# Decode attention and token mixer on one core: the order of the V loads that stay, and three resident V chunks ahead of K

## The chip, the cores and the metric

The kernel runs on one core of a Trainium2 chip, in one launch. The metric is the device time of that launch in microseconds (us), less is better; the time of a kernel is the median of its runs. The core's engines are called PE (matrix products), DVE (vector), ACT (scalar functions), POOL and SP; here SP only issues the loads, one after the other, each when its target cell is free.

## The reference

```python
def _A_ref(x, k_cache, v_cache, wq, wo):      # Hq = 32, Hkv = 8, Sk = 32768, Dh = 128, D = 512, B = 2
    q = (x @ wq).reshape(B, 1, 32, 128).transpose(0, 2, 1, 3)
    k, v = jnp.repeat(k_cache, 4, axis=1), jnp.repeat(v_cache, 4, axis=1)
    p = softmax(einsum("bhqd,bhkd->bhqk", q, k) * 128 ** -0.5)
    o = einsum("bhqk,bhkd->bhqd", p, v)
    return o.transpose(0, 2, 1, 3).reshape(B, 1, 4096) @ wo
def _B_ref(x, w1, b1, w2, b2):                 # S = 1 token, F = 1792
    u = gelu(einsum("bsd,sf->bdf", layernorm(x), w1) + b1)
    return (einsum("bdf,fs->bds", u, w2) + b2).transpose(0, 2, 1)

x = x + _A_ref(layernorm(x), k_cache, v_cache, wq, wo)
x = x + _B_ref(layernorm(x), w1, b1, w2, b2)
x = x + _A_ref(layernorm(x), k_cache, v_cache, wq, wo)   # the same caches and weights again
x = x + _B_ref(layernorm(x), w1, b1, w2, b2)
```

All in float32. The caches are 2 x 8 heads of 32768 x 128 for K and for V, and both layers read all of them.

## The kernel before

**Units and chunks.** A unit is one layer, one batch and one KV head: 32 of them, numbered 0 to 31 in the order of the list `units`. Each has 8 chunks of K and 8 of V; a chunk is 4096 keys, 128 partitions x 4096 floats, 2.097 MB. Head 7 is the keeper: parts of its K and V stay on the chip from layer 0 to layer 1. Unit 13 (N1) is layer 0, batch 0, head 7; unit 14 is layer 0, batch 1, head 5; unit 15 is layer 1, batch 0, head 7; unit 16 (N2) is layer 0, batch 1, head 7; unit 17 is layer 1, batch 0, head 5; unit 18 (N3) is layer 1, batch 1, head 7; unit 19 is layer 1, batch 1, head 5. At units 13 and 16 a batch's layer 0 ends (a "change"): the output goes through the mixer, and the query of a unit two later comes from it.

**The stream.** A list `stream` holds all loads with a key, and its sorted order is the order of everything: SP issues loads in it and PE takes the chunks in it, so K of one unit and V of the unit before are interleaved. A position is the number of chunks taken so far. `parts` (L857 on) says which chunks a load takes together; `FOLLOWS` (L34) gives V of units 15 and 18 their keys relative to K of the next unit. "K14 2" is chunk 2 of K of unit 14 below, "V1-3" chunks 1 to 3 of V.

**What stays.** `KEPT` gives, for each chunk of the keeper's V, how many of its 8 parts stay and the cell: chunks 1 to 3 in cells 8 to 10, chunks 5 to 7 in cells 3 to 5, and of chunk 4 five eighths in cell 13. The other three eighths of chunk 4 are loaded into a half cell; two of them are copied by DVE into two banks of PSUM (`kept`, L537) and in layer 1 copied back (L526), the third is loaded again. In layer 1, chunks 1 to 3 and 5 to 7 need no load ("resident").

**The cells.** Between units 12 and 19 the loads share the cells 0 to 10, each one chunk, with the weights in 9 to 12. For every load the planner (`spread`, `half`, `fit`, `room`) takes the cells with the largest lead (how many chunks are loaded between the position that frees them and this load, at most 4, and that no later booked use cuts off), and among equals those free first. After the V of units 13 and 16, with chunks 1 to 3 and 5 to 7 in their cells, the next K (L866, one chunk at a time from chunk 2) goes through four half cells, 6.0, 6.5, 7.0 and 7.5 (the number is cell and half), in turn. A half is free when PE has multiplied what was in it, and, where DVE copies from it, when that is done as well.

**The end of a unit.** With the last V chunk taken, DVE adds the blocks (L546, L548), PE turns them (L618), the output product follows (L245). At a change the rows are then copied (L632), go to PE (L664) and through a normalisation, and `hidden_sum` runs 14 tiles through ACT (L803) and DVE (L818, L820), one tile at a time; `mix_3` (L828) takes the sum to PE at the position after K chunk 6. PE works in program order, so these stand between K chunks.

**Scores.** K gives scores in PSUM, two halves of 4 chunks each. After the last K chunk: the maximum (L440, L446, L448, L450, L454, L456), a transposition of each half into `S` (L460), exponentials on ACT (L465), four for each half; V chunks 0 to 3 use the first half, 4 to 7 the second. The query of a unit is made by products (L339), a copy (L361) and a turn (L365) some positions ahead of its K; for unit 19 the copy goes to the memory of `S[0]`, so it stands ahead of the transposition of unit 18's first half, which the program puts 3 positions ahead of K19 at the earliest. `load_weights` (L118) brings two heads' weights in one load; for unit 20 it goes to cells 9 and 10, 7 positions ahead of K20.

Of the kernel before, what the change touches and what calls it, by code (L numbers as in the profile page):

```python
# [30 lines left out]
KEPT_Q = 4  # L31
RESIDENT = (5, 7)
TWO_HEADS = ((0, 1), (2, 3), (4, 6), RESIDENT)
FOLLOWS = {2: (2.2, -0.9, -0.8, -0.7, 3.5, -0.6, -0.5, -0.4), 5: (3.05, 1.1, 1.2, 1.3, 5.1, 3.1, 3.2, 3.3)}  # L34
PIECES = (32, 16, 8, 4, 4)
THIN = 16
QT = 4
# [7 lines left out]
def gqa_mixer_kernel(ctx: ExitStack, tc: tile.TileContext, x, kt, v, wqo, cols, out):  # L45
# [811 lines left out]
    def parts(n, with_v):  # L857

        m = n + with_v
        if m < N1 or n > N3 and m > N3 + 1:  # L860

            loads = ((0, 4), (4, 2), (6, 2)) if m == NU else ((0, 2), (2, 2), (4, 2), (6, 2)) if m == N3 + 2 else GROUPS
            return [(c, k, NCH) for c, k in loads]
        if not with_v:
            loads = ((0, 3), (3, 1), (4, 2), (6, 2)) if n in (N1, N2) else ((0, 2), (2, 2), (4, 2), (6, 2))
            if n in (N1 + 1, N2 + 1):  # L866
                loads = ((0, 2), *((c, 1) for c in range(2, NCH)))
            if n in (N1 + 2, N3):
                loads = [(c, 1) for c in range(NCH)]
        elif n in (N1, N2):  # L870
            loads = ((0, 1), (5, 3), (1, 3), (4, 1))
        elif n in (N1 + 1, N2 + 1):
            loads = [(c, 1) for c in range(NCH)]
        elif n < N1:
            loads = ((0, 2), (2, 2), (4, 2), (6, 2))
        else:
            loads = [(c, 1) for c in range(NCH)]
        return [(c, k, RING) for c, k in loads]

    stream = []  # L880
    for n in range(NU):
        stream += [(n * NCH + c + m - 1, 0, n, c, m, limit) for c, m, limit in parts(n, 0)]
        for i, (c, m, limit) in enumerate(parts(n, 1)):
            if n in (N1, N2):
                key = (n + 1) * NCH + 1 + (i + 1) / (2 * NCH)
            elif n in (N1 + 1, N2 + 1):
                key = (n + 1) * NCH - 0.5 + max(c / (2 * NCH) - 0.5, c - 2 + m)
            elif n - N1 in FOLLOWS:
                key = (n + 1) * NCH + FOLLOWS[n - N1][c]
            else:  # L890
                key = (n + 1) * NCH + c + m - 1 + (LAG if N1 - 1 <= n <= N3 else 0)
            stream.append((key, 1, n, c, m, limit))
# [215 lines left out]
```

## Time and profile before

| | us |
|---|---|
| median of 3 runs | 2496.51 |
| lowest and highest of them | 2495.5, 2499.65 |
| the profiled execution | 2498.0 |
| its span in the trace | 2496.2 |
| PE busy / DVE busy / ACT busy | 1374.8 / 240.2 / 187.4 |

The profile lists busy time by engine; groups of instructions by line; the chain of work that ended last, followed backwards from the last instruction; DMA queues; and, by windows, for each stretch the busy time of PE, PE's weight loads, DVE, ACT and POOL with the number of instructions, then PE's granted clock (1.00 is full speed), the mean busy share of the 16 DMA engines (short windows can show more than 1, since a packet counts where it ends) and GB/s. A row of the timeline is: start, duration, engine, line, operation, target and source, count, and in brackets the idle time before and what ended it. A row of the waits is: who waited for whom, total us, times, longest. A timeline row with a count merges several instructions; its duration is then the stretch from the first to the end of the last.

### The profile page before, as it was taken

The page shows a single profiled execution, that of the slowest core. Times are in us where ns is not written, and L with a number is a line of the kernel's source. Part 1 is how long each engine was busy: PE and PEld are TensorE (multiplying, and loading weights), DVE is VectorE, ACT ScalarE, POOL GpSimd, SP SyncE. Part 2 cuts the span into 40 slices and gives each one's busy share as a digit, 9 for nine tenths or more (in the row PEclk, how much of TensorE's full clock was granted, in tenths as well). Part 3 has the DMA queues.
Part 4 walks back from the last instruction along what each step waited for, and adds up shares of the span by engine and source line. Part 5 has one row for each costly group of instructions (what it writes and reads, how often), then busy time and mean ns, then how long its engine had stood idle before and what let it go on. Part 6 is the DMA issues. An engine that isn't in the chain of part 4 may idle for free.

```text
span 2496.2 us, 20457 instructions
## 1 busy us (share of the span) xinstructions
PE 1374.8 (55%) x9270; PEld 373.0 (15%) x9270; DVE 240.2 (10%) x632; ACT 187.4 (8%) x554; POOL 4.9 (0%) x17
## 2 busy tenths in 40 slices
PE   4545445645445544657677666465455464456546
PEld 1111111111111111111121111111111111111112
DVE  1000000000000000003113100000000000010002
ACT  0000000000000000002012000000000000011002
POOL 0000000000000000000000000000000000000000
PEclk8777767876777777778887887777778677777778
DMA  9999999999999999999999999999999999999996
GB/s 420 435 435 427 436 429 436 431 434 431 435 434 431 433 427 431 430 429 388 432 430 401 427 426 430 439 433 431 430 437 430 431 433 433 434 429 433 427 434 279
DMA packets 30336, 1063.04 MB, mean 426 GB/s; under 512 B 3621, under 2 KB 3625, under 8 KB 4522
## 3 DMA queue, kind: packets, MB, share of 16 engines
q1 hardware_dynamic: 29960, 1061.70, 99.0%
q8 instruction: 73, 1.20, 0.2%
q14 instruction: 13, 0.11, 0.0%
q10 hardware_dynamic: 290, 0.04, 0.0%
HBM read 1061.72 MB, written 0.00 MB: 425 GB/s over the span
## 4 chain that ended last, share of the span: by engine, by line
DMA 74%; PE 24%; another core or an unknown queue 0%; issue 0%; DVE 0%; ACT 0%; SPq 0%
DMA mem<-in_v_dram 63%; PE acc L578 19%; DMA mem<-in_kt_dram 12%; PE scores L425 3%; PE small L454 0%; PE small L609 0%; PE rows L245 0%; PE bcast L339 0%; PE small L448 0%; PE kept L760 0%; PE bcast L664 0%; PE bcast L640 0%; DVE S L548 0%; ACT S L465 0%
## 5 line engine op out<-in xcount | busy, mean ns | idle before, releaser
L425 PE MATMUL scores<-mem,small_sb 128*32 128x512 f32 x4096 | 634.8, 739 | 610.0 <-DMA mem<-in_kt_dram 609.9
L578 PE MATMUL acc<-mem,S 128*16 128x512 f32 x4088 | 601.4, 728 | 459.8 <-DMA mem<-in_v_dram 453.4
L425 PEld LDWEIGHTS scores<-mem,small_sb 128*32 128x32 f32 x4096 | 151.4, 129 | 999.2 <-issue 910.3
L465 ACT ACTIVATE S<-S,small_sb 128x128 f32<-128x128 f32 x240 | 123.3, 517 | 2105.5 <-DVE small_sb L456 1630.7
L578 PEld LDWEIGHTS acc<-mem,S 128*16 128x16 f32 x4088 | 133.1, 110 | 819.9 <-issue 694.1
L440 DVE TENSOR_REDUCE small_sb<-scores 128x1 f32<-128x512 f32 x64 | 44.2, 691 | 813.6 <-PE scores L425 813.6
L460 DVE STREAM_TRANSPOSE S<-scores 128x512 f32<-128x512 f32 x64 | 45.4, 710 | 114.6 <-PE acc L578 114.6
L339 PE MATMUL kept<-mem,small_sb 128*2 128x512 f32 x104 | 51.2, 618 | 1.7 <-DVE small_sb L273 1.7
L245 PE MATMUL rows<-mem,small_sb 128*1 128x512 f32 (+1 forms) x276 | 49.0, 605 | 2.6 <-ACT mem L803 2.4
L465 ACT ACTIVATION_READ_ACCUMULATOR S<-S,small_sb 128x1 f32 x240 | 44.8, 187 | 0.0
L611 DVE RECIPROCAL small_sb<-small 128x4 f32<-128x4 f32 x32 | 5.9, 184 | 322.9 <-PE small L609 322.9
L450 DVE TENSOR_REDUCE small_sb<-small 1x4 f32<-1x128 f32 x32 | 8.9, 279 | 277.7 <-PE small L448 277.7
L620 DVE TENSOR_TENSOR small_sb<-small,small_sb 128x4 f32<-128x4 f32 x31 | 5.1, 164 | 295.6 <-PE small L618 295.6
L548 DVE SCALAR_TENSOR_TENSOR S<-acc,small_sb,S 128x128 f32<-128x128 f32 x93 | 32.6, 351 | 3.3
L803 ACT ACTIVATE S<-bcast,small_sb 128x512 f32<-128x512 f32 x28 | 21.5, 777 | 95.4 <-DVE small_sb L672 93.3
L365 PE MATMUL small<-small_sb,mem 2*128 2x2 f32 x112 | 14.8, 250 | 17.9 <-DVE mem L361 17.9
L546 DVE TENSOR_SCALAR S<-acc,small_sb 128x128 f32<-128x128 f32 x31 | 10.8, 350 | 132.4 <-PE acc L578 132.4
L618 PEld LDWEIGHTS small<-small_sb,S 128*128 128x128 f32 x62 | 12.6, 254 | 48.5 <-issue 40.8
L339 PE MATMUL bcast<-mem,small_sb 128*1 128x512 f32 (+1 forms) x40 | 19.5, 603 | 0.0
L820 DVE SCALAR_TENSOR_TENSOR acc<-S,small_sb,acc 128x512 f32<-128x512 f32 x24 | 18.1, 755 | 2.5
L365 PEld LDWEIGHTS small<-small_sb,mem 2*128 2x128 f32 x112 | 13.7, 188 | 30.6 <-DVE mem L361 27.3
L448 PE MATMUL small<-small_sb 128*1 128x128 f32 x64 | 16.6, 353 | 1.5 <-DVE small_sb L446 1.3
(134 smaller groups left out, 267.3 us busy)
## 6 DMA issues: line engine op xcount, KB each, us to landing
mem<-in_kt_dram SPq DMA_DIRECT2D x14, 4096.0 KB, 24.8
mem<-in_v_dram SPq DMA_DIRECT2D x9, 4096.0 KB, 23.2
mem<-in_wqo_dram SPq DMA_DIRECT2D x7, 4096.0 KB, 37.6
mem<-in_kt_dram SPq DMA_DIRECT2D x12, 2048.0 KB, 21.0
mem<-in_v_dram SPq DMA_DIRECT2D x4, 6144.0 KB, 28.4
mem<-in_kt_dram SPq DMA_DIRECT2D x24, 1024.0 KB, 9.3
mem<-in_v_dram SPq DMA_DIRECT2D x11, 2048.0 KB, 20.2
mem<-in_v_dram SPq DMA_DIRECT2D x21, 1024.0 KB, 8.8
```

The costliest lines, as they stand in the source:

```text
L245: nc.tensor.matmul(rows[32 * g : 32 * g + b + 1, :], weights if b else weights[:, 1:], row, start=False, stop=True, skip_group_check=True,)
L339: nc.tensor.matmul(q_ps[n][:m, :], xnT[:, d, b : b + m], wq_at(h)[:, d, :], start=(d == 0), stop=(d == DT - 1),)
L365: nc.tensor.matmul(pt[:, r * m : (r + 1) * m], q_row[n][:m, r * DH : (r + 1) * DH], ident[:m, :m], start=True, stop=True,)
L425: nc.tensor.matmul(sc_ps[n, half][32 * g : 32 * g + 32, :], q, kc[k * NG + g], start=(i == 0 and k == 0), stop=(i == PACK - 1 and k == SUB ...
L440: nc.vector.tensor_reduce(mx[n][:, half : half + 1], sc_ps[n, half], axis=AX.X, op=ALU.max)
L448: nc.tensor.matmul(pm[:1, :P], mxa, ident, start=True, stop=True)
L460: nc.vector.transpose(S[half], sc_ps[n, half])
L465: nc.scalar.activation(s[:, :, h], s[:, :, h], AF.Exp, bias=neg[n][:, h : h + 1], scale=SCALE, accum_out=lsum[n][:, half, h : h + 1],)
L548: nc.vector.scalar_tensor_tensor(t, acc[:, k * DH : (k + 1) * DH], mask[:, k : k + 1], t, op0=ALU.mult, op1=ALU.add)
L578: nc.tensor.matmul(acc[32 * g : 32 * g + R * QT, :], S[half][:, col : col + R * QT], vc[q], start=(c == v_from[n] and q < NG), stop=(c == ...
L803: nc.scalar.activation(hid[key, f], px[key], AF.Gelu_apprx_tanh, bias=shift[key][:, f : f + 1], scale=slope[key][:, f : f + 1],)
L820: nc.vector.scalar_tensor_tensor(h if f == FT - 1 else acc, h, w, acc, op0=ALU.mult, op1=ALU.add)
```

## The change

Two tables of constants change, and with them the order and the cells, which follow from the planner's rules.

```diff
-FOLLOWS = {2: (2.2, -0.9, -0.8, -0.7, 3.5, -0.6, -0.5, -0.4), 5: (3.05, 1.1, 1.2, 1.3, 5.1, 3.1, 3.2, 3.3)}
+FOLLOWS = {2: (2.2, -0.9, -0.8, -0.7, 3.5, -0.6, -0.5, -0.4), 5: (3.05, 0.1, 0.2, 0.3, 5.1, 3.1, 3.2, 3.3)}
...
         elif n in (N1, N2):
-            loads = ((0, 1), (5, 3), (1, 3), (4, 1))
+            loads = ((0, 1), (1, 3), (4, 1), (5, 2), (7, 1))
```

In units 13 and 16 the V chunks were loaded and taken in the order 0, then 5 to 7 in one load, 1 to 3 in one load, and 4. Now it is 0, 1 to 3 in one load, 4, 5 and 6 in one load, and 7; each group is written (first chunk, count). All of them stand, as before, between K chunks 0-1 and 2 of the next unit.

In unit 18 the order around K of unit 19 was K19 0-1, V1-3, K19 2-3, V0, V5-7, K19 4-5, V4, K19 6-7. Now V1-3 (resident, no load) stands first, and the rest follows as it was. The query of unit 19 and the transposition of unit 18's first half of scores are placed relative to K19, so they move three positions later too.

## The prediction

> **What bounds the kernel now.** I read the page's head, its list of DMA queues and the shares of the chain that ended last, in that order.
>
> ```profile
> span 2496.2 us, 20457 instructions
> q1 hardware_dynamic: 29960, 1061.70, 99.0%
> DMA 74%; PE 24%; another core or an unknown queue 0%; issue 0%; DVE 0%; ACT 0%; SPq 0%
> ```
>
> One queue, SP's, moves 1061.70 MB and fills 99.0% of what the 16 DMA engines have; the chain that ended last is DMA for 74%. So the kernel lasts as long as its bytes, plus the time in which the DMA engines have too little queued. A microsecond of such a hole closed is a microsecond off the end, as long as no other hole opens. I therefore looked for holes: busy time, clock, DMA share and GB/s (the last two columns) by windows, first long ones, then of a few microseconds around the places the diff touches.
>
> ```profile
> 1500.00:1700.00 200.00, 107.60 (x673) 28.04 (x669) 13.70 (x38) 12.65 (x48) 0.00 (x0) 0.74 1.00 433
> 1200.00:1290.00 90.00, 62.76 (x442) 15.49 (x434) 9.93 (x26) 4.14 (x16) 0.00 (x0) 0.87 1.01 431
> 1145.00:1150.00 5.00, 4.23 (x42) 1.94 (x42) 1.40 (x4) 0.00 (x0) 0.00 (x0) 1.00 0.61 215
> 1157.00:1159.00 2.00, 0.36 (x4) 0.16 (x8) 1.77 (x3) 1.76 (x3) 0.00 (x0) 1.00 0.83 193
> 1338.00:1341.00 3.00, 2.23 (x22) 0.60 (x14) 1.40 (x4) 0.00 (x0) 0.00 (x0) 1.00 0.72 240
> 1348.00:1350.00 2.00, 0.49 (x8) 0.00 (x0) 1.62 (x3) 1.76 (x4) 0.00 (x0) 1.00 1.00 209
> 1447.00:1461.00 14.00, 13.93 (x130) 3.84 (x126) 2.76 (x5) 0.00 (x0) 0.00 (x0) 1.00 0.94 389
> ```
>
> The steady rate is 431 to 433 GB/s, so a chunk of 2.097 MB takes 4.87 us and a half 2.44. Against 431, five holes stand out: 5 x (431-215)/431 = 2.5 us and 2 x (431-193)/431 = 1.1 us after unit 13, 1.3 and 1.0 us after unit 16 by the same sum, and 14 x 42/431 = 1.4 us in unit 18. Two of them answer to one wait of SP, the last to another; next are SP's waits in three stretches, SP's issues, and the DVE copies that the first wait is for.
>
> ```profile
> SPq L139 <- DVE kept L537: 29.3, 1, 29.3
> SPq L139 <- DVE kept L537: 31.6, 1, 31.6
> SPq L118 <- PE acc L578: 19.5, 1, 19.5
> 1113.32 1.39 SPq L139 DMA_DIRECT2D mem<-in_kt_dram  x3
> 1142.66 1.29 DVE L537 COPY kept<-mem 128x512 f32<-128x512 f32 x2 [15.22 <-DMA mem<-in_v_dram]
> 1148.04 1.19 SPq L139 DMA_DIRECT2D mem<-in_kt_dram  x2
> 1154.85 1.19 SPq L139 DMA_DIRECT2D mem<-in_kt_dram  x2
> 1158.64 1.63 PE L425 MATMUL scores<-mem,small_sb 128*32 128x512 f32 x8 [1.77 <-DMA mem<-in_kt_dram]
> 1334.98 1.29 DVE L537 COPY kept<-mem 128x512 f32<-128x512 f32 x2 [16.35 <-DMA mem<-in_v_dram]
> 1339.20 0.33 SPq L139 DMA_DIRECT2D mem<-in_kt_dram  x1
> ```
>
> **The V order in units 13 and 16: what is removed.** By the planner's rules the second half of K chunk 3 of the next unit goes into half cell 6.0, where the rest of V chunk 4 lies. Chunk 4 is now the last V load. At 1113.32 SP issues three half chunks of K; the fourth waits until chunk 4 has landed (the copy starts at 1142.66), been copied and been multiplied, and goes out at 1148.04. At 1142.66 the queue held 1.5 chunks, 7.3 us, and was due to be empty at 1150.0; so at the issue 1.9 us were left, and 2.5 us were lost. In unit 16 the same sum gives 1334.98 + 7.3 = 1342.3, issue at 1339.20, 3.1 us left, 1.3 lost. Left and lost add up to 4.4 us both times. That is my measure: a load needs some 4.4 us still queued ahead of it, or the difference is lost.
>
> **What takes its place.** With the order 0, 1-3, 4, 5-6, 7 the planner's rules give these cells (a number in brackets is the stream position whose end frees them):
>
> - before, unit 13: K14 0-1 in 6-7 [214], V0 in 8 [214], V5-7 in 3-5 [212], V1-3 in 8-10 [219], V4 rest in 6.0 [218], K14 2 in 6.5 and 7.0, K14 3 in 7.5 and 6.0 [226]
> - after: K14 0-1 in 3-4 [212], V0 in 7 [214], V1-3 in 8-10 [214], V4 rest in 6.0 [216], V5-6 in 3-4 [218], V7 in 5 [216], K14 2 in 6.5 [216] and 7.0 [219], K14 3 in 7.5 [219] and 6.0 [223]
>
> The last number is the point: the half waits for position 223, not 226. V1-3 no longer waits for V0 either. Unit 16 is alike, with 271 in place of 274. The DVE copies (1.29 us) come three positions earlier in DVE's order; between them and the end of the unit no other DVE work is emitted, so nothing stands behind them. The bytes are the same; one load becomes two, an issue of 0.33 us on an SP that is waiting anyway. SP is now held at V5-6 until K14 0-1 is used (1109.4, the first row below), with V0, V1-3 and V4 queued behind that K, five chunks or 24 us of cover.
>
> Whether a hole opens further on is decided by PE, in order, at the end of the unit:
>
> ```profile
> 1107.11 2.24 PE L425 MATMUL scores<-mem,small_sb 128*32 128x512 f32 x16
> 1123.09 3.61 PE L578 MATMUL acc<-mem,S 128*16 128x512 f32 x16 [11.16 <-DMA mem<-in_v_dram]
> 1144.98 1.16 PE L640 MATMUL bcast<-small_sb 128*128 128x128 f32 x8
> 1146.07 1.91 PE L578 MATMUL acc<-mem,S 128*16 128x512 f32 x16
> 1147.79 1.04 PE L425 MATMUL scores<-mem,small_sb 128*32 128x512 f32 x8
> 1149.92 1.07 PE L425 MATMUL scores<-mem,small_sb 128*32 128x512 f32 x8
> 1153.72 1.92 PE L425 MATMUL scores<-mem,small_sb 128*32 128x512 f32 x16
> 1168.18 0.75 DVE L820 SCALAR_TENSOR_TENSOR S<-S,small_sb,acc 128x512 f32<-128x512 f32 x1
> 1171.13 1.12 PE L828 MATMUL bcast<-S,small_sb 128*128 128x512 f32 x2
> ```
>
> The same bytes are ahead, so the last V chunk (7 now) again lands at about 1142.7 and V5-6 at 1137.8. V5-6 takes 3.6 + 1.9 us of PE (cold, then warm, by the second and fourth row), the eight products of L640 1.1, V7 1.9: the unit ends at 1146.3, where it was 1148.0. From there the work of the end of the unit runs as it did: K14 2 in two parts, between them and after them the output products and the mixer's first ones, and K14 3 begins 5.7 us after the end of V (1153.72 - 1148.0). The halves of K14 land at 1145.1, 1147.6, 1150.0 and 1152.4. K14 4 goes out when the halves of K14 2 are used, at 1147.4 and 1149.3, with 5.0 and 5.5 us queued. K14 5 goes out when the first half of K14 3 is used, at 1146.3 + 5.7 + 1.0 = 1153.0, when the queue reaches to 1157.3: 4.3 us, just at the measure. The present run has a hole at that place too: 1154.85 against a landing at 1158.64 is 3.8 us, so 0.6 of the 1.1 us lost are this, and the rest is something else.
>
> So the first holes go, 2.5 + 1.3 = 3.8 us, and of the second ones 0.6 each at most, 1.2 us, of which I take 0.9 since the margin is nil (between 0 and the whole 2.1). The mixer's hidden sum must end before L828: it ends at 1168.93, and L828 runs at 1171.13, 2.2 us of cover. It starts with the end of V, 1.7 us sooner; the K stream comes 2.5 us sooner; 1.4 us of cover stay, and where they are gone PE holds the K and V behind it one for one.
>
> **A rule against the second term.** The 3.8 us above stand below my measure of 4.4 us. The Trainium skill, DMA: Bandwidth & Descriptors, section "Anatomy of one DMA — SWDGE (gpsimd) path", gives one DMA a fixed part of about 2.0 us beside its bytes, most of it the receipt of the last write; it says so of DMAs that GpSimd issues, and these are SP's. By that, an estimate from this page, 3.8 us queued are enough, the holes at 1157 and 1348 are no lack of queued loads, and the term is 0 and not 0.9. The trace doesn't agree: 3.1 us were queued in unit 16, and yet 1.3 us lost.
>
> **Unit 18.** Chunks 1 to 3 of V are resident, no load; they move ahead of K19 0-1 in PE's order. Moved with it, three positions later: the query of unit 19 (products L339, copy L361, turn L365; PE waits for data in that stretch) and the transposition of its first half of scores, which now stands behind the maximum.
>
> ```profile
> 1434.57 0.71 DVE L460 STREAM_TRANSPOSE S<-scores 128x512 f32<-128x512 f32 x1
> 1434.69 0.52 ACT L465 ACTIVATE S<-S,small_sb 128x128 f32<-128x128 f32 x1 [58.13 <-DVE small_sb L456]
> 1436.21 0.50 ACT L465 ACTIVATE S<-S,small_sb 128x128 f32<-128x128 f32 x1
> 1440.21 6.35 PE L425 MATMUL scores<-mem,small_sb 128*32 128x512 f32 x32 [5.75 <-DMA mem<-in_kt_dram]
> 1446.38 3.62 PE L578 MATMUL acc<-mem,S 128*16 128x512 f32 x32
> 1432.38 0.33 SPq L139 DMA_DIRECT2D mem<-in_v_dram  x1
> 1452.22 0.33 SPq L118 DMA_DIRECT2D mem<-in_wqo_dram  x1
> 1452.60 0.42 SPq L139 DMA_DIRECT2D mem<-in_kt_dram  x1
> ```
>
> SP issues nothing from 1432.38 to 1452.22, since the weights go where V chunks 2 and 3 lie. At 1432.38 five chunks or fewer were queued; K19 0-1 lands at 1440.2, three chunks more at 1454.8. So 2.6 us were left at 1452.2, 1.8 lost by the measure, 1.4 by the window. After: one transposition more (0.71) before the exponentials; the first four of the eight, those of the first half, end at 1436.9 now and would at 1437.7; PE is idle then, takes V1-3 in 3.6 + 1.9 + 1.9 = 7.4 us, and the weights go out at 1445.1, with 9.7 us queued. K19 0-1 follows, 3.9 us, to 1449.0, so K19 4-5, which now waits for position 301 where it was 298, goes out at 1449 where it stood behind the weights until 1452.6. Term: 1.4 at most, 0 at least if the exponentials came 7 us late; I take 1.2, nearest to the window.
>
> **Sum.** 3.8 + 0.9 + 1.2 = 5.9 us less of holes, 0.3 off for the mixer's thinner cover: 5.6 us. The profiled execution took 2498.0 us (span 2496.2, 1.8 around it) and would take 2492.4; it lies 1.5 us above the median of 2496.51, from which I predict 2490.9 us. A measurement of this kernel can tell some 0.2% or 5 us from no change, and the sum is hardly more.
>
> **The rivals.** (1) Only the two first holes and unit 18's go; the second ones are made by something the order doesn't touch. For it: a DMA share of 1.00 at 209 GB/s, engines busy with something else; against it: 0.83 at 193 GB/s. Gain 3.8 + 1.2 - 0.3 = 4.7, so 2491.8 us. The rule of the skill's page would come to this. (2) Given back: not the wait but the end of the unit on PE decides when the ring of four half cells turns. If V5-6 were through PE 2 us later than I have it, the four half loads of K14 4 and 5 would find 2.3 to 3.5 us queued, and 2 us more would go in each of the two units; gain 5.6 - 4 = 1.6, so 2494.9 us. For it: the margin of nil; against it: the rows of PE, in which nothing could take these 2 us. (3) Slower: SP stands at V5-6, which now needs cells 3-4 back from K14 0-1, and V7 and all of K14 stand behind it. The cover is 24 us less the measure, 19.6; from there on each microsecond that PE takes longer to K14 0-1 is lost in both units. With 25 us it is 2 x 5.4 - 5.6 = 5.2 us slower, 2501.7 us. For it: a wait that the order of before doesn't have, on an engine that takes turns with the output products and the mixer; against it: PE was through with that K at 1109.4, 33 us before the last V landed. (4) The change does nothing, since another wait holds the fourth half: 2496.5 us. The cells above speak against it.
>
> **How the numbers follow.** Forecast 0.56 (own range 2488.5 to 2492.5), rival 1 0.18, rival 2 0.13, rival 3 0.08, rival 4 0.05. The line of 0.2% is 2491.5: of the forecast 0.46 lies below it and 0.10 above; rival 1 stands on its edge, 0.08 below and 0.10 above; rivals 2 and 4 lie between it and 2501.5, rival 3 beyond. That makes 0.54 faster, 0.38 within, 0.08 slower. The lower end takes the full 7.3 us of all five holes and 1 us of a run's scatter, 2488.2; the upper takes rivals 2 and 4 and half a microsecond of scatter, 2497.0. The three runs shown lie from 2495.5 to 2499.65.
>
> **What would show it.** Right: SP's wait for the copy of L537 no longer the last before a hole, DMA rate above 400 GB/s in the 5 us after either V end, some 4 us of GB/s back there; the weights of L118 out about 7 us after the exponentials of unit 18 and not 18; K14 5 issued with more than 4 us queued. Wrong: a hole of the same size some microseconds further on, at L664 or L828; V1-3 of unit 18 starting later than 1440; or a rate that falls elsewhere.

## The result and the profile after

| | median, us | lowest, highest | runs |
|---|---|---|---|
| before | 2496.79 | 2494.9, 2499.66 | 12 |
| after | 2492.18 | 2491.1, 2493.0 | 12 |

The ratio is 0.998, with a 95% interval from 0.9971 to 0.9988: 4.6 us less, between 3.0 and 7.2. The profiled execution took 2493.0 us. First the page of the changed kernel, its head, SP's queue and the shares of the chain.

```profile
span 2491.1 us, 20467 instructions
q1 hardware_dynamic: 30248, 1061.70, 99.1%
DMA 74%; PE 24%; DVE 0%; issue 0%; another core or an unknown queue 0%; ACT 0%; SPq 0%; POOL 0%
```

The same bytes go through the same queue, 5.1 us sooner by the span; what changed is the time in which the DMA engines ran short. The windows of the changed kernel at the five holes, at 1154, and three long ones (the last two columns are the DMA share and GB/s):

```profile
1145.00:1150.00 5.00, 3.92 (x34) 0.92 (x26) 1.80 (x6) 0.00 (x0) 0.00 (x0) 1.00 0.95 367
1157.00:1159.00 2.00, 1.06 (x8) 0.16 (x8) 1.79 (x3) 1.84 (x3) 0.00 (x0) 1.00 0.97 406
1154.00:1156.00 2.00, 0.97 (x8) 0.19 (x8) 1.03 (x2) 1.79 (x3) 0.00 (x0) 1.00 0.81 295
1338.00:1341.00 3.00, 2.24 (x18) 0.67 (x18) 0.81 (x3) 0.00 (x0) 0.00 (x0) 1.00 1.02 423
1348.00:1350.00 2.00, 0.57 (x12) 0.03 (x4) 1.77 (x3) 1.84 (x3) 0.00 (x0) 0.80 1.00 418
...
1140.00:1160.00 20.00, 14.07 (x108) 3.70 (x100) 9.01 (x19) 5.38 (x8) 0.54 (x1) 0.98 0.99 389
1332.00:1352.00 20.00, 14.56 (x108) 3.73 (x100) 10.31 (x21) 6.72 (x9) 0.54 (x1) 0.93 1.01 419
1366.00:1380.00 14.00, 12.69 (x95) 3.82 (x96) 5.73 (x11) 1.26 (x2) 0.00 (x0) 0.99 0.96 391
1447.00:1461.00 14.00, 11.67 (x108) 2.94 (x100) 2.58 (x4) 0.00 (x0) 0.00 (x0) 1.00 1.02 435
```

And the same three long windows of the kernel before:

```profile
1140.00:1160.00 20.00, 16.48 (x124) 4.36 (x116) 8.44 (x19) 3.48 (x5) 0.54 (x1) 0.93 0.90 346
1332.00:1352.00 20.00, 16.19 (x120) 4.23 (x112) 9.18 (x20) 4.24 (x6) 0.54 (x1) 0.93 0.96 367
1366.00:1380.00 14.00, 12.59 (x84) 3.44 (x84) 7.15 (x14) 1.26 (x2) 0.00 (x0) 1.00 1.01 415
```

By the prediction's sum, length x (431 - rate) / 431, the twenty microseconds around the end of unit 13 lost 3.9 us and lose 1.9; those around the end of unit 16 lost 3.0 and lose 0.6. That is 4.4 us regained. At 1366 to 1380, where unit 17's scores follow the mixer of unit 16, 0.5 us became 1.3, so 0.8 went back. The hole of unit 18 is gone (389 to 435 GB/s).

SP's waits of the changed kernel answer to the prediction's first and third row (who waited for whom: total, times, longest):

```profile
SPq L139 <- DVE kept L537: 12.6, 2, 6.3
SPq L118 <- PE acc L578: 12.5, 1, 12.5
```

Before, each was the last wait ahead of a hole: 29.3 and 31.6 us for the copy, 19.5 for the weights. Now the two are some 6.3 us each, and the weights 12.5. The rows of the timeline, in order, from the end of unit 13 to unit 18:

```profile
1132.56 0.33 SPq L139 DMA_DIRECT2D mem<-in_kt_dram  x1
1142.83 1.16 PE L640 MATMUL bcast<-small_sb 128*128 128x128 f32 x8
1143.92 1.91 PE L578 MATMUL acc<-mem,S 128*16 128x512 f32 x16
1145.64 1.04 PE L425 MATMUL scores<-mem,small_sb 128*32 128x512 f32 x8
1146.74 2.48 SPq L139 DMA_DIRECT2D mem<-in_kt_dram  x2
...
1151.57 1.97 PE L425 MATMUL scores<-mem,small_sb 128*32 128x512 f32 x16
1152.69 0.33 SPq L139 DMA_DIRECT2D mem<-in_kt_dram  x1
...
1166.03 0.75 DVE L820 SCALAR_TENSOR_TENSOR S<-S,small_sb,acc 128x512 f32<-128x512 f32 x1
1167.91 1.94 PE L425 MATMUL scores<-mem,small_sb 128*32 128x512 f32 x8 [0.55 <-DMA mem<-in_kt_dram]
1169.78 2.06 PE L828 MATMUL bcast<-S,small_sb 128*128 128x512 f32 x2
...
1434.47 0.53 ACT L465 ACTIVATE S<-S,small_sb 128x128 f32<-128x128 f32 x1 [60.27 <-DVE S L460]
1436.64 7.65 PE L578 MATMUL acc<-mem,S 128*16 128x512 f32 x48 [3.09 <-ACT S L465]
1444.36 0.33 SPq L118 DMA_DIRECT2D mem<-in_wqo_dram  x1
```

The fourth half of K14 3 goes out at 1132.56, and not at 1148.04: 15 us sooner, and 17 us ahead of 1150.0, where the queue of before would have run empty. The unit ends on PE at 1143.92 + 1.91 = 1145.8, and K14 4 goes out as soon as the first half of K14 2 is used (1145.64 + 1.04, then 1146.74). The wait that comes after the one removed is therefore PE's end of the unit, and at 1145 to 1150 it still costs 0.7 us.

### The profile page after: what moved, and what is told of

It is laid out like the page before. It is cut to its first block, busy times and chain, and to the rows that moved or that the text cites. A ratio compares the mean times of both kernels' runs of the same rounds, so it can differ in the third digit from the quotient of the medians.

```text
span 2491.1 us, 20467 instructions
## 1 busy us (share of the span) xinstructions
PE 1368.1 (55%) x9270; PEld 371.9 (15%) x9270; DVE 240.1 (10%) x632; ACT 187.5 (8%) x554; POOL 4.9 (0%) x17
## 4 chain that ended last, share of the span: by engine, by line
DMA 74%; PE 24%; DVE 0%; issue 0%; another core or an unknown queue 0%; ACT 0%; SPq 0%; POOL 0%
DMA mem<-in_v_dram 65%; PE acc L578 20%; DMA mem<-in_kt_dram 9%; PE scores L425 3%; PE bcast L339 0%; PE small L454 0%; PE small L609 0%; PE small L448 0%; PE rows L245 0%; PE kept L760 0%; PE bcast L640 0%; DVE S L548 0%; ACT S L465 0%; PE bcast L828 0%
## 5 line engine op out<-in xcount | busy, mean ns | idle before, releaser
L425 PE MATMUL scores<-mem,small_sb 128*32 128x512 f32 x4096 | 627.5, 732 | 608.5 <-DMA mem<-in_kt_dram 608.5
L820 DVE SCALAR_TENSOR_TENSOR acc<-S,small_sb,acc 128x512 f32<-128x512 f32 x24 | 18.1, 755 | 2.5
```

The lines of the kernel that those rows point to most:

```text
L425: nc.tensor.matmul(sc_ps[n, half][32 * g : 32 * g + 32, :], q, kc[k * NG + g], start=(i == 0 and k == 0), stop=(i == PACK - 1 and k == SUB ...
L820: nc.vector.scalar_tensor_tensor(h if f == FT - 1 else acc, h, w, acc, op0=ALU.mult, op1=ALU.add)
```

## The experiments

Each line is one kernel, timed beside the kernel before on the same chip; the median of before was 2496.79, 2497.55, 2497.45, 2497.33 and 2497.34 us in groups 0 to 4. "Trace" is the gain in the three long windows above, in one profiled execution, against the 7.4 us that before's own lost there (3.9 + 3.0 + 0.5); it does not hold unit 18.

| group | kernel | median | against before | ratio, interval | trace |
|---|---|---|---|---|---|
| 0 | changed, the result above | 2492.18 | -4.6 | 0.9971 to 0.9988 | 3.6 |
| 1 | V order alone | 2492.67 | -4.9 | 0.9974 to 0.9992 | 1.7 |
| 1 | `FOLLOWS` alone | 2496.85 | -0.7 | 0.9990 to 1.0008 | 1.3 |
| 1 | 0, 1-3, 5-7, 4 | 2497.20 | -0.3 | 0.9994 to 1.0012 | -1.2 |
| 1 | 0, 1-3, 5-6, 4, 7 | 2492.50 | -5.0 | 0.9971 to 0.9989 | 4.4 |
| 2 | mixer's products early | 2496.16 | -1.3 | 0.9986 to 1.0004 | 0.9 |
| 2 | changed, PE kept busy | 2491.92 | -5.5 | 0.9972 to 0.9990 | 4.2 |
| 2 | 0, 1-3, 5-6, 4, 7 and new `FOLLOWS` | 2491.87 | -5.6 | 0.9971 to 0.9989 | 4.1 |
| 2 | the same, PE kept busy | 2492.20 | -5.2 | 0.9972 to 0.9989 | 4.2 |
| 3 | 0, 1-3, 5-6, 7, 4 | 2493.03 | -4.3 | 0.9977 to 0.9994 | 4.2 |
| 3 | 0, 4, 1-3, 5-7 | 2500.78 | +3.5 | 1.0005 to 1.0023 | -4.3 |
| 3 | changed, again | 2491.72 | -5.6 | 0.9969 to 0.9986 | 2.9 |
| 4 | changed, mixer's row later | 2492.27 | -5.1 | 0.9971 to 0.9989 | 4.0 |

**Each part alone.** The first two kernels have one of the two lines of the change and the other as before.

> The V order of units 13 and 16 as changed, FOLLOWS as before. My theory (the half of K that waits for chunk 4's use made the hole, and the rest of the gain is in unit 18): 3.0 to 3.8 us faster than before, span holes after the V end of units 13 and 16 gone, SP's silence in unit 18 still there (weights about 20 us after the load ahead of them). Rival (the two edits are one gain, in the V order alone): 4.6 us faster, and nothing left for unit 18.

> Only FOLLOWS as changed, the V order as before. My theory: 1.0 to 1.4 us faster than before, the weights of L118 out some 7 us sooner after the exponentials, holes after units 13 and 16 as before. Rival (unit 18's hole is filled again later): no change, 0.0 +- 0.5 us.

The V order alone has 4.9 us, where the changed kernel has 4.6 and 5.6 in its two measurements. That is above the 3.0 to 3.8 expected, and by the time alone the rival, one gain in the V order, fits as well. `FOLLOWS` alone, 0.7 us, is not told from nothing by its times, and neither is what it adds to the order 0, 1-3, 5-6, 4, 7 (5.6 against 5.0). The traces help a little: from the start of K18 7 on PE to that of K20, both set by their landing, the seven kernels with the old `FOLLOWS` took 83.5 to 84.7 us, mean 84.3, and the seven with the new one 83.3 to 84.5, mean 83.6. So it is worth about 0.7 us, less than the prediction's 1.2; the two groups overlap, so the size is rough.

**What of the V order does it.** The first kernel moves 5-7 behind 1-3 and leaves chunk 4 last. The second puts chunk 4 next to last.

```diff
-            loads = ((0, 1), (5, 3), (1, 3), (4, 1))
+            loads = ((0, 1), (1, 3), (5, 3), (4, 1))
```

```diff
-            loads = ((0, 1), (5, 3), (1, 3), (4, 1))
+            loads = ((0, 1), (1, 3), (5, 2), (4, 1), (7, 1))
```

> Order 0, 1-3, 5-7, 4 in units 13 and 16, so chunk 4 stays last but V1-3 needn't wait for V0 and the cells are those of the change; FOLLOWS as before. My theory: the fourth half of K still waits for position 226, so the hole stays and the time is that of before, 0.0 +- 0.7 us. Rival (what helps is the earlier cells of V1-3 and K14, or the order of the two three-chunk loads): 2 to 3.5 us faster as in the V order alone.

> Order 0, 1-3, 5-6, 4, 7; FOLLOWS as before. The half waits for position 225, one before the end and not three. My theory (only the last place hurts, since left and lost add up to 4.4 us): as the V order alone, 3.0 to 4.2 us faster, the fourth half issued about 9 us before the queue is empty. Rival (each of the three positions is worth a third): 1.0 to 1.5 us faster.

With chunk 4 last nothing is gained. Its window at the first hole, and, from the timeline, the copy, PE's part of chunk 4 and SP's issue of the half:

```profile
1145.00:1150.00 5.00, 4.35 (x40) 1.59 (x32) 1.33 (x4) 0.00 (x0) 0.00 (x0) 1.00 0.54 188
```

```profile
1142.74 1.29 DVE L537 COPY kept<-mem 128x512 f32<-128x512 f32 x2 [15.17 <-DMA mem<-in_v_dram]
1146.58 1.91 PE L578 MATMUL acc<-mem,S 128*16 128x512 f32 x16
1148.55 1.19 SPq L139 DMA_DIRECT2D mem<-in_kt_dram  x2
```

The waits put SP's wait down to the DVE copy, but the copy ends at 1142.74 + 1.29 = 1144.03, and the half goes out at 1148.55, when PE is through with chunk 4 (1148.49). PE is the releaser here: it came to chunk 4 late, 3.8 us after it had landed, because a load of three chunks stood before it. With chunk 4 next to last the half is out at 1139.92, the rate at 1145 to 1150 is 375 GB/s, and the gain of 5.0 us is above the 3.0 to 4.2 expected.

These two leave open whether chunk 4's place counts, or only how late PE is at the end. Two more kernels take the two apart: finer loads with chunk 4 still last, and chunk 4 early with three chunks in one load last.

```diff
-            loads = ((0, 1), (5, 3), (1, 3), (4, 1))
+            loads = ((0, 1), (1, 3), (5, 2), (7, 1), (4, 1))
```

```diff
-            loads = ((0, 1), (5, 3), (1, 3), (4, 1))
+            loads = ((0, 1), (4, 1), (1, 3), (5, 3))
```

> The order of before with finer loads and chunk 4 still last: 0, 1-3, 5-6, 7, 4, FOLLOWS old. The theory (what counts is how much is queued when the fourth half of K14 3 goes out, not the place of chunk 4): V7 alone ends on PE at about 1140.3, L640 behind it at 1141.4, so PE is free when chunk 4 lands at 1142.7; copy to 1143.95, products to 1144.6, and the half goes out at about 1144.7 with 1150.0 - 1144.7 = 5.3 us queued, above what was lost against in any trace so far (4.4 to 5.0). So the hole at 1145 to 1150 is gone, SP's wait before it is short, and the time is as with the V order alone: 4 to 5.5 us below before, about 2492.7. Rival (chunk 4's place in the order is what counts, and last means late): the half at 1147 to 1148.5, a rate below 300 GB/s at 1145 to 1150, and the time of before within 1.3 us, as with the order 0, 1-3, 5-7, 4.

> The other way round: chunk 4 early, but three chunks in one load last: 0, 4, 1-3, 5-7, FOLLOWS old. The half of K14 3 that waited for chunk 4 is free long before it is needed (its position is 220). The theory: the load of 5-7 lands whole at about 1142.7, PE then needs 3.6 + 1.9 + 1.9 us and 1.1 for L640, so the unit ends at about 1151.2, 3 us later than before; the halves of K14 2 and 3 are all loaded by 1152.4 and K14 4 can go out only at about 1152.3, with nothing left: 4.4 us or more lost per unit, where before lost 2.5 and 1.3 at the first place and 1.1 and 1.0 at the second. Time 0 to 5 us above before, about +2. Rival (once chunk 4 is not last, the gain is there whatever comes last): 4 to 5.5 us below before. What is left of the queue at the issue of K14 4, and the rate from 1150 to 1160 tell them apart.

The theory held in both. The first, finer loads and chunk 4 last, by its copy, PE's part of chunk 4 and SP's issue in the timeline, and its window:

```profile
1142.81 1.29 DVE L537 COPY kept<-mem 128x512 f32<-128x512 f32 x2 [15.27 <-DMA mem<-in_v_dram]
1141.10 2.77 PE L578 MATMUL acc<-mem,S 128*16 128x512 f32 x16
1144.16 0.33 SPq L139 DMA_DIRECT2D mem<-in_kt_dram  x1
```

```profile
1145.00:1150.00 5.00, 3.61 (x22) 0.95 (x26) 0.63 (x3) 0.00 (x0) 0.00 (x0) 0.76 0.98 385
```

PE is not behind, the copy (to 1144.10) really is the last releaser, and the half goes out with 1150.1 - 1144.2 = 5.9 us queued (the copy's start and 7.3): no hole of the old size, 4.3 us faster, though chunk 4 stands last. The second, chunk 4 early and three chunks last, by the same two views (5-7, the last products, SP's issue of K14 4):

```profile
1142.58 5.45 PE L578 MATMUL acc<-mem,S 128*16 128x512 f32 x32 [6.95 <-DMA mem<-in_v_dram]
1149.04 1.91 PE L578 MATMUL acc<-mem,S 128*16 128x512 f32 x16
1151.87 0.33 SPq L139 DMA_DIRECT2D mem<-in_kt_dram  x1
```

```profile
1145.00:1150.00 5.00, 5.00 (x44) 1.86 (x40) 0.00 (x0) 0.00 (x0) 0.00 (x0) 0.87 0.65 272
1150.00:1155.00 5.00, 4.05 (x38) 0.96 (x30) 1.67 (x6) 0.00 (x0) 0.00 (x0) 1.00 0.55 202
```

PE idles 6.95 us until the large load is whole, ends the unit at 1150.95, and K14 4 goes out at 1151.87 with half a microsecond queued. 4.5 us are lost in these ten, and the kernel is 3.5 us slower than before. The gain is thus not chunk 4's place; it is that PE is not late at the end, since no load of three chunks stands last or, as before the change, next to last.

**PE's end of the unit.** This kernel keeps the order of before and does L640, which stands ahead of chunk 4 on PE, three positions earlier.

```diff
-            at(vend - 1 if change else vend, mix_1, key)
+            at(vend - 4 if change else vend, mix_1, key)
```

> The kernel before, with the mixer's eight products of L640 (1.16 us on PE, ahead of V chunk 4 in PE's order) put three positions earlier, where PE waits for V1-3. Chunk 4 is through PE 1.1 us sooner; the DVE copy of L537 ends when it did. My theory (the half of K waits for PE's use of chunk 4, and left and lost add up to 4.4 us): the half is issued 1.1 us sooner, about 1146.9 and 1338.1, each hole is 1.1 us smaller, 2.2 us faster than before. Rival (the wait is for the copy, as the profile names it): the issue stays at 1148.0 and 1339.2, 0.0 +- 0.7 us.

The half went out 0.7 us sooner, at 1147.32, just behind PE's end of chunk 4 at 1147.25, while its copy ended at 1143.87 as before. So PE is the releaser, and L640's 1.1 us count for 0.7 of it. The copy starts at 1142.58, so the queue reaches to 1149.9 and 2.6 us were left; by the measure of 4.4 the hole should have shrunk to 1.8 us. It is still

```profile
1145.00:1150.00 5.00, 4.22 (x42) 1.17 (x38) 1.57 (x5) 0.00 (x0) 0.00 (x0) 1.00 0.67 247
```

in the window of this kernel, 2.1 us lost in the five, 2.4 from 1144 to 1150 (before lost 2.5 in either). Left and lost make 5.0 here. The kernel is 1.3 us faster than before, where 2.2 were expected; its interval, 0.9986 to 1.0004, doesn't tell that from nothing, so the rows and not the time show that PE is waited for.

**The clock behind the mixer.** In the changed kernel's first profile L828 and the K chunks around it run at half clock (2.06 us for L828 where before had 1.12), and the rate falls at 1180 and 1370. Two kernels give PE three small products into unread memory at five half positions there, to keep it at full clock: the changed kernel, and the order 0, 1-3, 5-6, 4, 7 with the new `FOLLOWS`. That order without the additional products is the third.

```diff
                 at(vend + 4.5, highest, n + 1, 0)
+                for j in range(5, 10):
+                    at(vend + j / 2, idle_products, 3, rank=2)
```

> The changed kernel, with three extra products of 128x128 into scratch after each half chunk of K between positions 2.5 and 4.5 after the end of V in units 13 and 16, where PE waits for data; their result isn't read. My theory (what the V order wins is partly given back where PE runs at half clock at L828, the query's products and V0 of the next unit): PE clock 1.00 from there on, the holes at 1180 and 1370 smaller, 0.5 to 2 us faster than the changed kernel, so 5.1 to 6.6 us faster than before. Rival (these holes are the chain of maxima and query itself, whatever the clock): as the changed kernel, 4.6 us faster than before, +- 0.7.

> Order 0, 1-3, 5-6, 4, 7 together with FOLLOWS as changed. My theory (the two edits add up): 0.5 to 1.3 us faster than the same order with FOLLOWS as before, so 5.5 to 6.3 us faster than before. Rival (unit 18's hole is only there in some executions, so the median doesn't show it): 5.0 us faster, +- 0.5.

> The run before this one (order 0, 1-3, 5-6, 4, 7, FOLLOWS as changed) with the extra products of the warm ring. My theory: another 0.5 to 2 us faster than without them, 6 to 8 us faster than before. Rival (the chain, not the clock): the same as without them, +- 0.7.

In the trace of the first the clock is 1.00 at 1160 to 1175 and the rate at 1366 to 1380 is 410 GB/s, where it was 391. In the times it is nothing: 5.5 us faster than before, against 5.6 and 4.6 in the changed kernel's two measurements, and 5.2 against 5.6 for the other order. The 0.8 us given back at 1370 are seen in the traces, but that this clock sets the end was a theory that fell. Two traces with L828 at full clock speak against it as well: before has a fall like that at 1180 too, at 1183 to 1185 (209 GB/s), and the V order alone, with 1.12 us for L828 in both units, has the deepest fall near 1370.

**The same kernel again, and the second hole.** The changed kernel once more; and the changed kernel with L664 and the hidden sum half a position later.

```diff
-            at(vend + (1 if change else 3), mix_2, key)
+            at(vend + (1.5 if change else 3), mix_2, key)
...
-                at(vend + 1, hidden_sum, key)
+                at(vend + 1.5, hidden_sum, key)
```

> The changed kernel once more, beside these two and the same runs of before. 2492.2 within 0.7, ratio 0.9979 to 0.9983. It gives a second profile of the same program: if the holes near 1180 and 1370 and the clock at L828 differ from the first profile, they belong to an execution and not to the change; if they are the same, to the change.

> The changed kernel, with the row's product for the mixer (L664, and the hidden sum behind it) half a position later, so that the first half of K chunk 3 of the next unit goes through PE ahead of it. In the changed kernel that half is taken at 1151.57, after L664, and K14 5 goes out at 1152.69; the rate then dips at 1154 to 1156 (238 and 352 GB/s, 0.6 us lost). The theory (the second hole is a lack of queued loads): the half is taken at 1150 to 1150.6, K14 5 goes out 1 to 1.6 us sooner, 1151.1 to 1151.7, and the dip at 1154 to 1156 is gone (each of the two us above 400 GB/s); L664 runs at 1151 to 1151.6, the hidden sum ends at 1167.3 to 1167.9, and L828 stays at 1169 to 1170. The time is 0.5 to 1 us below the changed kernel's, less than medians tell apart: about 2491.2. Rival (the dip is made by something the order doesn't touch, for example the engines' other work): K14 5 sooner and the dip as it was, the time the changed kernel's.

The second profile of the same program, by its windows, and SP's first issue of K14 4 in its timeline:

```profile
1137.00:1143.00 6.00, 5.42 (x28) 1.17 (x32) 0.00 (x0) 0.00 (x0) 0.00 (x0) 0.50 0.99 415
1145.00:1150.00 5.00, 4.22 (x38) 1.18 (x38) 1.57 (x5) 0.00 (x0) 0.00 (x0) 1.00 0.80 310
...
1370.00:1372.00 2.00, 2.00 (x24) 1.09 (x16) 0.38 (x2) 0.00 (x0) 0.00 (x0) 1.00 0.81 254
```

```profile
1147.72 0.33 SPq L139 DMA_DIRECT2D mem<-in_kt_dram  x1
```

and the first profile's window of V5-6:

```profile
1137.00:1143.00 6.00, 5.36 (x33) 1.16 (x34) 0.00 (x0) 0.00 (x0) 0.00 (x0) 0.72 0.99 415
```

The dip at 1370 comes back (254 GB/s; 209 in the first profile, 422 in before's), and the V order alone has it too (360 at 1366 to 1380), so it is not one execution's; with PE kept busy (410), or with the mixer's row later (411), the same 14 us hardly show it. Nor is it a mark of the new order: 0, 1-3, 5-7, 4, which gained nothing, has 387 there. The rest of the first hole differs: V5-6 ran at a mean clock of 0.50 and not 0.72, the unit ended 1 us later, K14 4 went out at 1147.72 and not 1146.74, and the rate at 1145 to 1150 is 310 and not 367 GB/s, 1.4 us lost instead of 0.7.

With the mixer's row later, PE's rows and SP's issue of K14 5 in the timeline, and the window:

```profile
1150.68 1.04 PE L425 MATMUL scores<-mem,small_sb 128*32 128x512 f32 x8
1151.68 1.13 PE L664 MATMUL bcast<-S,small_sb 128*128 128x512 f32 x2
1151.78 0.33 SPq L139 DMA_DIRECT2D mem<-in_kt_dram  x1
```

```profile
1154.00:1156.00 2.00, 0.92 (x8) 0.19 (x8) 0.47 (x3) 0.78 (x2) 0.54 (x1) 1.00 1.03 410
```

K14 5 goes out 0.9 us sooner, though the unit ended 1.2 us later in this execution (V7 ends at 1146.99, the clock again 0.50), and at 1154 to 1156 295 GB/s became 410 (377 and 442 in its two halves, where more than 400 in each was expected). Some of the dip moved forward, so a longer window is the fairer measure: from 1152 to 1158 the rate is 391 GB/s here, 0.6 us lost, against 371 in the first profile of the changed kernel, 0.8 lost, and 358 in the second, 1.0 lost, where K14 5 went out at 1153.67. The second profile is the nearer partner, since its first hole was about as large (310 GB/s against 298). So the second hole was in good part a lack of queued loads. The times don't show it (2491.2 us expected, 2492.27 measured); half a microsecond is less than they tell.

No kernel beat the changed one by more than the measurement tells. The order 0, 1-3, 5-6, 4, 7 does the same.

## Why the prediction was right

The direction, the mechanism and the range held: 2490.9 us forecast, 2492.18 measured. Of the 1.3 us between them 0.3 are the median of before, 2496.51 of three runs and 2496.79 of twelve; 1.0 is the gain, 5.6 forecast and 4.6 measured (5.6 when measured again). The chance of 0.54 was on a gain beyond 0.2%; at 0.18% it came out just short of that line, and at 0.22% just beyond it when measured again. The time alone would fit rival 1, with a gain of 4.7, better than the forecast; it is the windows that tell them apart. By steps:

- **The fourth half** no longer waits for the end of the unit: right. It went out 15 us sooner, and the holes that it made, 2.5 and 1.3 us, shrank to 0.7 (1.4 in the second profile) and to 3 x (431 - 423) / 431 = 0.1.
- **The term of the V order**, 3.8 + 0.9 - 0.3 = 4.4: 4.9 measured alone, and 4.4 by the first profile's windows at the two places, of which 0.8 went back at 1370. That the sum fits so well is in part luck: of the first holes' 3.8 some 3.0 came, of the second holes' 2.1 some 1.3 and not 0.9. The return at 1370 stood in none of the prediction's sums.
- **"A load needs some 4.4 us still queued ahead of it"**: the mis-sized rule. Two holes gave the same sum, 4.4, and it was carried on as a constant. That they agreed was luck, as other traces show. With L640 early it was 5.0. `FOLLOWS` alone, with the old V order, gives 2.8 + 1.8 = 4.6 in unit 13, but in unit 16 the copy starts at 1331.73, the half goes out at 1337.24 with 1.8 left, and 1.3 are lost (318 GB/s at 1336 to 1341): 3.1. At K14 4 of the changed kernel 1152.4 - 1146.7 = 5.7 us were queued and 0.7 were lost; in the second profile 4.7, and 1.4 lost; in the order 0, 1-3, 5-6, 4, 7 even 1152.4 - 1146.2 = 6.2, and 0.65 lost. The prediction took K14 4, "with 5.0 and 5.5 us queued", to be safe, and in unit 13 it was not. In unit 16 it was: K17 4, by SP's issue and PE's first products with it, landed 7.8 us after its issue, of which 2.4 are its own, so some 5.3 us were queued, and from 1336 to 1341 the rate was 421 GB/s. The need thus lies between some 3 us and more than 6, and what sets it in one place was not found. The two rows of K17 4:

```profile
1337.34 0.33 SPq L139 DMA_DIRECT2D mem<-in_kt_dram  x1
1345.09 1.06 PE L425 MATMUL scores<-mem,small_sb 128*32 128x512 f32 x8 [1.01 <-DMA mem<-in_kt_dram]
```

- **The end of the unit** on PE, 1146.3 forecast, was 1145.8 and 1146.8 in the two profiles: V5-6 took less or more of its time at half clock than the 3.6 + 1.9 us assumed.
- **The second holes**, 0.9 of 2.1: K14 5 was to go out at 1153.0 and did at 1152.69. The place in unit 16 is full (418 GB/s); in unit 13 0.6 us stay at 1154 to 1156. That they are a lack of queued loads, doubted by rival 1, is borne out by the later mixer's row, though in one execution and for part of the dip. The rule of the Trainium skill weighed there, DMA: Bandwidth & Descriptors, "Anatomy of one DMA — SWDGE (gpsimd) path", about 2.0 us of fixed time, would by the prediction's estimate have 3.8 us be enough. These runs speak against that estimate for SP's loads, since 4.7 us were not.
- **The mixer's thinner cover**, 0.3 off: it was not needed. The last L820 ends at 1166.78, the K chunk ahead of L828 on PE at 1169.85; the cover is 3 us, and L828 waits for K, as before.
- **Unit 18**, 1.2: mis-sized, about 0.7. Its steps came as described: V1-3 from 1436.64 (1437.7 forecast; the first exponential starts behind the first transposition and not behind both), the weights at 1444.36 (1445.1). The size was read from one hole in one execution, 389 GB/s at 1447 to 1461. In six other traces with the old `FOLLOWS` the same window had 397 to 428 GB/s; the mean of all seven, 411, is 14 x (431 - 411) / 431 = 0.65 us (0.9 against 440, the mean of the seven with the new one): there was half to two thirds as much to be had as that profile showed.
- **The rivals.** 1, a second hole that the order doesn't touch, fell: 1.3 of the 2.1 us went with the order, and K14 5 issued sooner took some of the rest. 2, given back at the end of the unit: the place was right, and the kernel 0, 4, 1-3, 5-7 shows its size where the unit does end late, but here it took 0.7 to 1.4 us in unit 13 and 0.1 in unit 16, and not 4. 3, SP held at V5-6: it cost nothing. V5-6 went out at 1109.34, when K14 0-1 had been used, and landed 28 us later. 4 fell: the half did wait for chunk 4 and PE.

**How far a trace can be trusted, and what stays open.** By the three windows the V order alone gained 1.7 us in its profiled execution, and 4.9 in the median of its runs. The two don't contradict each other, since a trace is of one execution. That of the V order alone took 2495.01 us, 2.3 above its median; before's took 2498.0, 1.2 above. Between these two lie 3.0 us, and with unit 18's window (389 GB/s in before, 428 here, 1.3 us) the four windows give 3.0. In the same way the four windows come within 1.1 us of the difference of the profiled executions in all thirteen profiles. So the windows account for most of the difference between two executions, but those of one kernel lie 2 to 6 us apart from the lowest to the highest (2491.26 to 2495.72 for the V order alone), and a term under a microsecond can't be read from one trace. Why they differ so, and why the rate dips near 1370 in some of them, was not found.

## What to carry to other kernels

In a kernel bound by DMA, take every issue that can be late, and compare what is queued at that moment with what the holes of several traces show (here between 3 and 6 us were needed), not with one hole's figure. Keep large loads away from the end of a stage, the last place and the one before it: when one stands there, the consumer idles until it is whole and then has all of it to do, while the buffers for the next loads are held. Before paying for a hole, see in a second profile whether it is as large there, and compare a trace with the time of its own execution, not with a median.

## What was not expected of the hardware

PE's clock in one and the same stretch differs between executions of the same instructions: at 1137 to 1143 it was 0.72 in the first profile of the changed kernel and 0.50 in the second, in which the unit ended 1 us later and the rate behind it was 310 instead of 367 GB/s. Three more traces have the same V order, and all five fall into one ranking: mean clocks of 0.50, 0.50, 0.55, 0.72 and 0.72 go with unit ends at 1147.0, 1146.8, 1146.7, 1145.8 and 1145.6 and with 298, 310, 346, 367 and 370 GB/s at 1145 to 1150. So the clock of an engine that isn't the bottleneck sets how much of a hole is left. The Trainium skill, TensorE: Matmul & The Clock Gate, "What's actually happening", says that the clock follows a window of 3413 ns that runs freely and doesn't begin with the kernel. The traces agree. These are the half microseconds in which the half clock begins and ends around V5-6, two of the first profile and two of the second:

```profile
1137.50:1138.00 0.50, 0.35 (x4) 0.15 (x8) 0.00 (x0) 0.00 (x0) 0.00 (x0) 0.56 0.90 377
1140.50:1141.00 0.50, 0.50 (x4) 0.00 (x0) 0.00 (x0) 0.00 (x0) 0.00 (x0) 0.53 1.02 426
```

```profile
1136.00:1136.50 0.50, 0.00 (x0) 0.00 (x0) 0.00 (x0) 0.00 (x0) 0.00 (x0) 0.68 0.54 229
1143.00:1143.50 0.50, 0.50 (x8) 0.00 (x0) 0.00 (x0) 0.00 (x0) 0.00 (x0) 1.00 0.99 410
```

With 1.00 before and behind and 0.50 between them, the half clock lasts from 1137.56 to 1140.97, 3.4 us, in the first, and from 1136.18 to 1143.0, 6.8 us, in the second: once and twice that window.

The waits of the profile named the DVE copy as what SP waited for, 29.3 us, though it had ended 4.1 us before the issue (1142.66 + 1.29 against 1148.04); with a wait for two engines the named one need not be the last, and only the rows of both tell.
